# A third depth for bursts of value products in a planned two-layer attention kernel

## The chip, the cores and the metric

The kernel runs on one core of a Trainium2 chip. The metric is the device time in microseconds of one execution; the kernel before takes 1564.23 us in the median of 3 runs (1563.62 to 1565.77).

## What is computed

Two rounds of attention and MLP over 2048 tokens of width 512, with the same weights in both rounds. Attention has 32 heads of width 16, so the score matrix is large for the little that each head computes: 32 x 2048 x 2048 exponentials in each round.

```python
def _A_ref(x, wqkv, wo):               # S = 2048, D = 512, H = 32, Dh = 16
    qkv = (x @ wqkv).reshape(B, S, 3, H, Dh).transpose(2, 0, 3, 1, 4)
    q, k, v = qkv[0], qkv[1], qkv[2]
    scores = einsum("bhqd,bhkd->bhqk", q, k) * Dh ** -0.5
    o = einsum("bhqk,bhkd->bhqd", softmax(scores), v)
    return o.transpose(0, 2, 1, 3).reshape(B, S, D) @ wo

def _B_ref(x, w1, b1, w2, b2):         # F = 1376
    return gelu(layernorm(x) @ w1 + b1) @ w2 + b2

x = x + _A_ref(layernorm(x), wqkv, wo)
x = x + _B_ref(layernorm(x), w1, b1, w2, b2)
# and both once more; inputs and weights are bf16
```

## The kernel before

**The work.** Each round's attention is cut into segments: a block of up to 512 queries times a group of four heads. A segment's scores are made in tiles of 128 keys x 512 queries for one head (`score`, L1466 to L1471): K is the stationary operand, and as a head fills only 32 rows of the array, four heads sit side by side in four row tiles. There are 4,096 such tiles in the program. A tile becomes probabilities in one of two ways:

- ScalarE (ACT) takes a group of three or two tiles and writes `exp` into the buffers `PT` (L1455). Groups alternate between PSUM banks 0 to 2 and 3 to 4, so that one group is computed while the other is read.
- VectorE (DVE) turns a tile into the bits of an exponential by adding a constant and converting to a 16-bit integer, into `dp` (L1555). It adds three shifted copies, two tiles at a time (L1588), and the four are averaged by multiplying with V scaled to match. Such a tile makes four value products instead of one. Only key blocks 3, 6, 9, 12 and 15 may go this way.

The value products (`try_pv`, L1605 to L1664) multiply probabilities with V (17 columns: 16 of the head and one of ones for the denominator). Four heads sit in four column tiles of the array, all adding into PSUM bank 6 (`ACCB`). Scores need the array in row tiles, value products in column tiles, projections and MLP the whole array; PE goes from one to the other in turns. When a segment's products are all in, DVE transposes the bank (L1688), and the next segment may start to add.

**Who sets the order.** The program is made by a planner, in Python, before anything runs: `Sched` keeps pending tasks for each engine, estimates when each could start, and emits them one by one with priorities. Scores have priority 0.0, value bursts 1.0. `best` and `scores_due` hold back a task of lower priority on PE when it would end later than scores that ACT will soon need, by `HOLD_LATE`. After the planning, `refill` puts matmuls on zeros (L1359, L1361, L1363) into PE's gaps to keep its clock up.

**A value burst.** `try_pv` looks at the products that are ready or will be within `PV_NEAR`, sorts them by column tile, and picks a depth r, the number of products per column tile in this burst, by the largest value. The burst goes out if the value reaches `PV_LEAST`, if score groups lack a `PT` buffer (`starved`), if the segment's last products are there, or if PE will have stood idle for half a microsecond. At most two bursts wait on PE at a time.

```python
value = lambda r: sum(min(r, len(v)) for v in by.values()) / (4.0 * (r + PV_COST))
r = max(range(1, PV_DEEP + 1), key=value)
if value(r) < HINT.PV_LEAST and not self.starved and len(near) < sg["n"] - sg["sub"]:
```

**The settings.** Class `Hint` (L506 to L519) holds a base setting and variations of it, one field or so in each. `ORDER` is a string of digits, one for every eight score groups: `flow_scores` (L1387) counts groups in `gi` and calls `HINT.at(gi // 8)`, which resets the base and applies the variation of that digit. So the string steers, stretch by stretch, when tiles go to DVE (`D_IDLE`, `D_STEAL`), how full a value burst must be (`PV_LEAST`), how early products count as ready (`PV_NEAR`), how far scores may be delayed (`HOLD_LATE`), and the priority of the second half of projections (`LIN2`). The depth limit `PV_DEEP` is a constant, 2.

Of the kernel before, what the change touches and what calls it, by code (L numbers as in the profile page):

```python
# [267 lines left out]
def I(fn, reads=(), writes=(), dur=0.3, same_ok=(), lat=None):  # L268
    return (fn, tuple(reads), tuple(writes), tuple(same_ok), dur, lat)
# [230 lines left out]
MISCB = 7  # L500
DTAIL = 8
DURGE = 8
PV_DEEP = 2
PV_COST = 0.5
PV_IDLE = 0.5


class Hint:
    BASE = dict(D_IDLE=1.2, PV_LEAST=0.75, HOLD_LATE=0.4, PV_NEAR=0.7, LIN2=9, D_STEAL=0)
    MODES = (dict(), dict(D_IDLE=0.8), dict(D_IDLE=1.7), dict(PV_LEAST=0.6), dict(PV_LEAST=0.9), dict(HOLD_LATE=0.2), dict(HOLD_LATE=0.6), dict(PV_NEAR=0.4), dict(LIN2=0.9), dict(D_STEAL=1.0))  # L510
    STEP = 8
    ORDER = '0355550015621021500127723542380000551183094330404202738042440023535555121020004212005090903453421320027044075009578104471100282939255971103200420580357499912000'

    def mode(self, k):
        self.__dict__.update(self.BASE)
        self.__dict__.update(self.MODES[k])

    def at(self, step):
        self.mode(int(self.ORDER[step], 36) if step < len(self.ORDER) else 0)  # L519


HINT = Hint()
# [3 lines left out]
class Builder:  # L526
# [1078 lines left out]
    def try_pv(self):  # L1605
        S_ = self.S_
        while True:
            if self.acc_seg >= len(self.segs) or not self.acc_free:
                return
            sg = self.segs[self.acc_seg]  # L1610
            if self.pv_out >= (1 if self.pv_first else 2) or not sg["rdy"]:
                return
            near = [it for it in sg["rdy"] if self.P.last_writer[it[2]].t1 <= S_.now + HINT.PV_NEAR]
            if len(near) < len(sg["rdy"]):
                S_.seq += 1
                heapq.heappush(S_.timers, (min(self.P.last_writer[it[2]].t1 for it in sg["rdy"] if it not in near) - HINT.PV_NEAR + 0.01, S_.seq, self.try_pv))
            if not near:
                return
            by = defaultdict(list)
            for it in near:  # L1620
                by[sg["tiles"][it[1]][1]].append(it)
            value = lambda r: sum(min(r, len(v)) for v in by.values()) / (4.0 * (r + PV_COST))
            r = max(range(1, PV_DEEP + 1), key=value)
            if value(r) < HINT.PV_LEAST and not self.starved and len(near) < sg["n"] - sg["sub"]:
                t = self.P.drain + PV_IDLE
                if S_.now < t or self.pv_out:
                    if not self.pv_timer:
                        self.pv_timer = True
                        S_.seq += 1
                        heapq.heappush(S_.timers, (max(t, S_.now) + 0.01, S_.seq, self.pv_again))  # L1630
                    return
            turns = [[v[k] for v in by.values() if len(v) > k] for k in range(r)]
            pick = [it for turn in turns for it in turn]
            for it in pick:
                sg["rdy"].remove(it)
            sg["sub"] += len(pick)
            nfirst = len(sg["first"])
            ops = []
            nth = {}
            for k, turn in enumerate(turns):  # L1640
                for it in turn:
                    nth[it[1], it[5]] = k
            for (s_, j, res, ap, use, sh) in pick:
                kbs, hp = sg["tiles"][j]
                hg, W, q = sg["hg"], sg["W"], sg["qslot"]
                first = hp not in sg["first"]
                sg["first"].add(hp)
                if first and sg["nparts"] == 2:
                    first = False
                    ops.append((nth[j, sh] - 0.1, I(lambda e, hp=hp, q=q: e.matmul(self.ps[32 * hp:32 * hp + 18, ACCB, :], lhsT=self.rsel[:, hp, :], rhs=self.QT[:, q, :], start=True, stop=False, skip_group_check=True, tile_position=(0, 32 * hp)),  # L1650
                                                     [("rsel",), ("qt", q)], [("ps", ACCB)], W / 2400.0, [("ps", ACCB)], ("col", hp))))
                for i, kb in enumerate(kbs):
                    if sh:
                        d = sg["dks"].index(kb) + sg["doff"]
                        v, RV = self.vs[:, q, sh - 1, d, 17 * hp:17 * hp + 17], ("vs", q, d)
                    else:
                        v, RV = self.V[:, hg, kb, hp, :], ("V", hg, kb)
                    ops.append((nth[j, sh] + 0.1 * i, I(lambda e, hp=hp, v=v, ap=ap[:, i * W:(i + 1) * W], first=first and i == 0, W=W: e.matmul(  # L1658
                        self.ps[32 * hp:32 * hp + 17, ACCB, 0:W], lhsT=v, rhs=ap, start=first, stop=False, skip_group_check=True, tile_position=(0, 32 * hp)),
                                     [res, RV], [("ps", ACCB)], W / 2400.0, [("ps", ACCB)], ("col", hp))))  # L1660
            ops = [o for i, o in sorted(ops, key=lambda x: x[0])]
            self.pv_first = nfirst < 4
            self.pv_out += 1
            S_.submit(Task("pe", 1.0, ops), cb=lambda sg=sg, pick=pick: self.pv_done(sg, pick))  # L1664
# [354 lines left out]
```

## Time and profile before

| what | from the profile of the kernel before |
|---|---|
| span of the profiled run | 1564.7 us, 39,699 instructions |
| exp groups on ACT (L1455) | 1,273, 1433.7 us: 590 of three tiles (1515 ns) and 683 of two (1086 ns, some overlap) |
| tiles on DVE (L1555) | 960, mean 679 ns |
| shifted copies on DVE (L1588) | 1,428 of 1,024 columns, mean 430 ns, and 24 of 512 |
| score matmuls (L1470) | 4,608 |
| value products (L1658) | 7,857 |
| zero matmuls (L1359, L1361, L1363) | 487, 465 and 1,808 |
| DMA | 24.9% of 16 engines' time on the main queue |

The page gives the busy time of each engine: PE for matmuls and PEld for their weight loads, DVE, ACT, POOL. "L1455 ACT ... idle before <-PE ps L1470" reads: the instructions of line 1455 found ACT idle before them, and what they waited for in the end was a matmul of line 1470. The chain that ended last is followed back from the last instruction, each step to what released it. A turn is here a run of matmuls in one tiling of the array, row tiles, column tiles or the whole, until the next turn's first matmul.

### The profile page before, as it was taken

To read this page: it belongs to the slowest core of one execution; us is meant where nothing else is said; L and a number is where in the kernel's file an instruction comes from. 1 tells how busy PE (TensorE), PEld (TensorE's weight loads), DVE (VectorE), ACT (ScalarE), POOL (GpSimd) and SP (SyncE) were. 2 spreads that over 40 slices of the span, in tenths; PEclk is the share of its full clock that TensorE was granted. 3 is DMA by queue.
4 is the path that set the end of the run, shared out by engine and by line. 5 is a ranking of instruction groups with operands and counts; after the bars stand their busy time and mean duration, and the time that the engine had idled before them with its cause. 6 is when DMAs were issued, how large, how long until landed. Compare 5 with 4: busy or idle time off the path is not lost.

```text
span 1564.7 us, 39699 instructions
## 1 busy us (share of the span) xinstructions
PE 1517.7 (97%) x16674; PEld 483.1 (31%) x16674; DVE 1459.9 (93%) x3256; ACT 1517.1 (97%) x1361; POOL 321.2 (21%) x558
## 2 busy tenths in 40 slices
PE   9999999999999999999999999999999999999998
PEld 3222222232223222222222322222232232344444
DVE  7699999999999899989999799999899999999894
ACT  8979999999999999999999999999999999999996
POOL 3575312001210021203222227410001000020100
PEclk9999999999999999999999999999999999999999
DMA  7663111203311232223832232310102000211110
GB/s 162 116 143 97 35 31 32 61 17 85 85 40 46 47 76 59 61 48 92 145 45 66 56 82 63 62 25 22 35 16 44 22 17 25 41 45 32 43 30 19
DMA packets 212451, 88.69 MB, mean 57 GB/s; under 512 B 183307, under 2 KB 207152, under 8 KB 212272
## 3 DMA queue, kind: packets, MB, share of 16 engines
q1 hardware_dynamic: 212272, 86.16, 24.9%
q8 instruction: 130, 2.13, 0.6%
q14 instruction: 49, 0.40, 0.1%
HBM read 34.65 MB, written 19.48 MB: 35 GB/s over the span
## 4 chain that ended last, share of the span: by engine, by line
ACT 34%; DVE 33%; PE 29%; issue 2%; POOL 1%; SPq 1%; DMA 1%; POOLq 0%; DVEq 0%
ACT PT L1455 33%; DVE dp L1555 13%; DVE dp L1588 10%; PE ps L1470 9%; PE ps L1658 8%; PE ps L1835 3%; PE ps L1792 2%; PE ps L950 2%; DVE accT L1688 2%; DVE n L1015 1%; ACT h L1827 1%; PE ps L1359 1%; DVE sq L991 1%; DVE h L1816 1%; PE ps L1068 1%
## 5 line engine op out<-in xcount | busy, mean ns | idle before, releaser
L1455 ACT ACTIVATE PT<-ps 128x1536 bf16<-128x1536 f32 (+1 forms) x1273 | 1433.7, 1285 | 28.5 <-PE ps L1470 25.1
L1555 DVE TENSOR_SCALAR dp<-ps 128x512 uint16<-128x512 f32 x960 | 638.1, 679 | 36.7 <-PE ps L1470 34.2
L1470 PE MATMUL ps<-QT,KT 32*128 32x512 bf16 (+1 forms) x4608 | 599.1, 359 | 19.6 <-ACT PT L1455 6.8
L1588 DVE TENSOR_SCALAR dp<-dp 128x1024 uint16<-128x1024 uint16 (+1 forms) x1452 | 559.9, 427 | 4.6 <-PE ps L1658 1.6
L1658 PE MATMUL ps<-PT,V 128*17 128x512 bf16 (+1 forms) x3525 | 483.8, 358 | 0.2 <-ACT PT L1455 0.2
L1658 PE MATMUL ps<-dp,vs 128*17 128x512 bf16 (+1 forms) x3249 | 467.6, 357 | 0.9 <-DVE dp L1588 0.4
L1470 PEld LDWEIGHTS ps<-QT,KT 32*128 32x128 bf16 x4608 | 161.1, 91 | 545.9 <-ACT PT L1455 286.3
L1196 POOL TENSOR_SCALAR QT<-qraw,scl,qbias 128x512 bf16<-128x512 bf16 (+1 forms) x83 | 72.3, 872 | 764.6 <-PE ps L1470 758.1
L1658 PE MATMUL ps<-dp,V 128*17 128x512 bf16 (+1 forms) x1083 | 227.1, 358 | 1.6 <-DVE accT L1688 0.6
L1363 PE MATMUL ps<-zw 128*32 128x448 bf16 (+23 forms) x1808 | 172.2, 321 | 0.8 <-DVE dp L1555 0.7
L1658 PEld LDWEIGHTS ps<-dp,vs 128*17 128x17 bf16 x3249 | 119.1, 88 | 115.4 <-issue 87.2
L1658 PEld LDWEIGHTS ps<-PT,V 128*17 128x17 bf16 x3525 | 116.9, 88 | 92.8 <-issue 78.5
L1361 PE MATMUL ps<-zw 32*128 32x444 bf16 (+5 forms) x465 | 132.8, 317 | 0.0
L1359 PE MATMUL ps<-zw 128*128 128x448 bf16 (+17 forms) x487 | 114.7, 334 | 3.2 <-DVE onec L754 2.1
L1792 PE MATMUL ps<-yT,wf 128*128 128x512 bf16 (+3 forms) x396 | 101.7, 361 | 3.1 <-DVE dp L1588 1.3
L950 PE MATMUL ps<-wqkv,xnT 128*128 128x512 bf16 x336 | 93.4, 382 | 5.8 <-DVE dp L963 2.2
L1363 PEld LDWEIGHTS ps<-zw 128*32 128x32 bf16 x1808 | 62.5, 95 | 27.8 <-DVE dp L1555 4.6
L1658 PEld LDWEIGHTS ps<-dp,V 128*17 128x17 bf16 x1083 | 55.5, 88 | 41.4 <-issue 24.1
L1221 POOL TENSOR_SCALAR vs<-V 128x340 bf16<-128x340 bf16 (+2 forms) x72 | 61.8, 859 | 26.1 <-PE ps L1658 15.1
L1688 DVE STREAM_TRANSPOSE accT<-ps 128x512 f32<-128x512 f32 (+1 forms) x88 | 57.8, 657 | 7.1 <-PE ps L1658 7.0
L1816 DVE TENSOR_SCALAR h<-ps,b1c 128x512 bf16<-128x512 f32 (+2 forms) x88 | 61.9, 703 | 1.9 <-PE ps L1792 1.5
L1359 PEld LDWEIGHTS ps<-zw 128*128 128x128 bf16 x487 | 37.6, 98 | 64.7 <-issue 40.0
(182 smaller groups left out, 885.5 us busy)
## 6 DMA issues: line engine op xcount, KB each, us to landing
vs<-vs_scr SPq DMA_DIRECT2D x56, 255.0 KB, 2.7
wf<-in_B_w_dram SPq DMA_DIRECT2D x90, 128.0 KB, 2.9
q_scr<-qk SPq DMA_DIRECT2D x20, 256.0 KB, 2.1
k_scr<-qk SPq DMA_DIRECT2D x12, 256.0 KB, 2.0
out_dram<-xres SPq DMA_DIRECT2D x16, 128.0 KB, 1.8
vs_scr<-vs SPq DMA_DIRECT2D x8, 255.0 KB, 2.9
xres<-in_A_x_dram SPq DMA_DIRECT2D x7, 256.0 KB, 3.2
v_scr<-vst SPq DMA_DIRECT2D x12, 136.0 KB, 1.7
```

Of the source, the lines that this page charges most:

```text
L950: yield Task("pe", prio if c0 == 0 else min(prio, HINT.LIN2), [I(lambda e, c=c: e.matmul(self.ps[:, b, :], lhsT=xnT[:, c, :], rhs=self.wqk ...
L1359: fn = lambda e: e.matmul(self.ps[:, b, 0:w], lhsT=self.zw[:, 0:128], rhs=self.zw[:, 0:w], start=st, stop=st, skip_group_check=True)
L1361: fn = lambda e: e.matmul(self.ps[:, b, 0:w], lhsT=self.zw[32 * p:32 * p + 32, 0:128], rhs=self.zw[32 * p:32 * p + 32, 0:w], start=st, sto ...
L1363: fn = lambda e: e.matmul(self.ps[32 * p:32 * p + 32, b, 0:w], lhsT=self.zw[:, 0:32], rhs=self.zw[:, 0:w], start=st, stop=st, skip_group_c ...
L1455: S_.submit(Task("act", 1e-5 * gi, [I(lambda e, pt=pt, n=n, b0=b0: e.activation(out=self.PT[:, pt:pt + n, :], in_=self.ps[:, b0:b0 + n, :] ...
L1470: return [I(lambda e, kb=kb, i=i: e.matmul(self.ps[:, b, i * W:(i + 1) * W], lhsT=self.KT[32 * hp:32 * hp + 32, hg, kb * 128:(kb + 1) * 12 ...
L1555: self.S_.submit(Task("dve", 0.0, [I(lambda e: e.tensor_scalar(out=self.dp[:, u, w * 512:(w + 1) * 512], in0=self.ps[:, b, :], scalar1=BIT ...
L1588: yield Task("dve", pr, [I(lambda e, k=k, v=v: e.tensor_scalar(out=self.dp[:, v, 0:N], in0=self.dp[:, u, 0:N], scalar1=float(SHIFT[k]), sc ...
L1658: ops.append((nth[j, sh] + 0.1 * i, I(lambda e, hp=hp, v=v, ap=ap[:, i * W:(i + 1) * W], first=first and i == 0, W=W: e.matmul(self.ps[32 ...
L1688: yield Task("dve", 0.3, [I(lambda e: e.transpose(self.accT[:, a, 0:W], self.ps[:, ACCB, 0:W]), [("ps", ACCB)], [RA], 0.17 + 0.535 * W / 5 ...
L1792: yield Task("pe", pr if c0 == 0 else min(pr, HINT.LIN2), [I(lambda e, c=c: e.matmul(self.ps[0:M, b, off:off + W], lhsT=self.w1(fc, c), rh ...
L1816: S_.submit(Task("dve", pr - 0.7, [I(lambda e, fc=fc, M=M, b=b: e.tensor_scalar(out=hv[0:M, fc * W:(fc + 1) * W], in0=self.ps[0:M, b, 0:W] ...
```

## The change

The depth limit becomes one of the fields that a setting may change. The base keeps 2. Two settings are added: a (a depth of 3), and b (a depth of 3, and a burst must reach a value of 0.84). The digits are read in base 36, so a and b need no new reading. The string of settings is a new one; its first 15 characters are as before, and from there on 127 of 145 differ. Twelve are a and fifteen are b. A burst of three per column tile lets PE change between row and column tiles less often.

```diff
-PV_DEEP = 2
 PV_COST = 0.5
 PV_IDLE = 0.5
 
 class Hint:
-    BASE = dict(D_IDLE=1.2, PV_LEAST=0.75, HOLD_LATE=0.4, PV_NEAR=0.7, LIN2=9, D_STEAL=0)
-    MODES = (dict(), dict(D_IDLE=0.8), dict(D_IDLE=1.7), dict(PV_LEAST=0.6), dict(PV_LEAST=0.9), dict(HOLD_LATE=0.2), dict(HOLD_LATE=0.6), dict(PV_NEAR=0.4), dict(LIN2=0.9), dict(D_STEAL=1.0))
+    BASE = dict(D_IDLE=1.2, PV_LEAST=0.75, HOLD_LATE=0.4, PV_NEAR=0.7, LIN2=9, D_STEAL=0, PV_DEEP=2)
+    MODES = (dict(), dict(D_IDLE=0.8), dict(D_IDLE=1.7), dict(PV_LEAST=0.6), dict(PV_LEAST=0.9), dict(HOLD_LATE=0.2), dict(HOLD_LATE=0.6), dict(PV_NEAR=0.4), dict(LIN2=0.9), dict(D_STEAL=1.0), dict(PV_DEEP=3), dict(PV_DEEP=3, PV_LEAST=0.84))
     STEP = 8
-    ORDER = '0355550015621021500127723542380000551183094330404202738042440023535555121020004212005090903453421320027044075009578104471100282939255971103200420580357499912000'
+    ORDER = '035555001562102a7b002a10378140b0a9b4400b2720a3048043b939400a433b43a0040b145523b7a110030b029922bb701ab0305733aa8531874000a09424434b380315000205ba188933009b003120'
...
-            r = max(range(1, PV_DEEP + 1), key=value)
+            r = max(range(1, HINT.PV_DEEP + 1), key=value)
```

## The prediction

> **What bounds the kernel now.** I read the profile from the outside in: the busy shares, then the span cut in three, then who waits for whom in the middle piece, then the chain of waits there.
>
> The first part of the page and the two lines of its chain:
>
> ```profile
> PE 1517.7 (97%) x16674; PEld 483.1 (31%) x16674; DVE 1459.9 (93%) x3256; ACT 1517.1 (97%) x1361; POOL 321.2 (21%) x558
> ...
> ACT 34%; DVE 33%; PE 29%; issue 2%; POOL 1%; SPq 1%; DMA 1%; POOLq 0%; DVEq 0%
> ACT PT L1455 33%; DVE dp L1555 13%; DVE dp L1588 10%; PE ps L1470 9%; PE ps L1658 8%; PE ps L1835 3%; PE ps L1792 2%; PE ps L950 2%; DVE accT L1688 2%; DVE n L1015 1%; ACT h L1827 1%; PE ps L1359 1%; DVE sq L991 1%; DVE h L1816 1%; PE ps L1068 1%
> ```
>
> Three engines are nearly full and the chain hops between them in equal parts, so no single one "is" the bound. PE's 97% contains zero matmuls that keep it warm (L1359, L1361, L1363: 115, 133 and 172 us, partly beside real work), so PE has slack in the sum, though not at every moment. ACT has none to speak of: it idles 47 us in all.
>
> Where? The setting of the burst depth is read anew every eight score groups from a string of 160 characters, and the new string first differs at character 15, so at group 120. In the trace the 120th exp (counted from 0) starts at 158.2 us. The last exp ends at 1543.6 us. So I cut there (columns: stage, length, then busy time of PE, weight loads, DVE, ACT, POOL, the clock, the DMA share, GB/s):
>
> ```profile
> 0.00:158.00 158.00, 148.47 (x1210) 46.29 (x1214) 133.27 (x310) 142.23 (x149) 85.54 (x179) 1.00 0.60 128
> 158.00:1543.60 1385.60, 1352.83 (x15364) 427.49 (x15360) 1320.71 (x2934) 1367.91 (x1200) 234.18 (x375) 1.00 0.22 49
> 1543.60:1564.70 21.10, 16.42 (x108) 9.30 (x108) 5.88 (x13) 7.01 (x14) 1.48 (x4) 1.00 0.04 13
> ```
>
> The head of 158 us can't change, and the tail of 21.1 us is a fixed string of projection, norm and MLP after the last segment. In the middle ACT idles 1385.6 - 1367.9 = 17.7 us and DVE 64.9 us. That is all there is to be won without cutting work. Who ends these waits, in the middle piece (us in total, times, longest):
>
> ```profile
> PEld ps L1470 <- ACT PT L1455: 260.1, 671, 0.9
> ...
> DVE dp L1555 <- PE ps L1470: 33.3, 50, 2.8
> ...
> ACT PT L1455 <- PE ps L1470: 14.1, 33, 2.4
> ...
> DVE dp L1588 <- PE ps L1658: 1.6, 7, 0.3
> ```
>
> The scores' weight load mostly waits for an exp to free its banks: ACT sets the pace. ACT itself waits for scores only 33 times, DVE 50 times. The last line is important for the buffers: DVE almost never waits for value products to free a `dp` buffer, and no line has ACT waiting for a value product at all.
>
> One gap is of another kind. Between 1213.0 and 1217.5 us the granted clock is 0.62 and ACT is busy 2.37 of 4.5 us:
>
> ```profile
> 1213.00:1217.50 4.50, 4.06 (x27) 1.00 (x27) 2.12 (x5) 2.37 (x3) 0.77 (x1) 0.62 0.00 0
> ```
>
> **What a burst costs.** Where PE is on the chain, the turns can be read off it (start, us, what):
>
> ```profile
> 1098.24 0.32 PE ps L1470 x3
> 1098.56 0.54 PE ps L1658 x8
> 1099.10 0.32 PE ps L1470 x3
> 1099.43 0.54 PE ps L1658 x8
> 1099.97 0.54 PE ps L1835 x2
> ```
>
> and elsewhere on it
>
> ```profile
> 337.38 0.97 PE ps L1658 x16
> ```
>
> Eight products (two per column tile) take 0.54 us from start to the next turn, sixteen take 0.97 us, so a level of four costs 0.215 us and a change of turn 0.11 us. The trace also has 14 unmixed turns of twelve, median 0.76 us, just on that line. Three per tile therefore occupies PE for 0.76 us instead of 0.54.
>
> **What the Trainium skill says.** "TensorEngine Tiling (Array Packing)", section Key Properties: a change of tiling mode, not of tile alone, drains the engine. The trace agrees, 0.11 us a change, which is the whole mechanical ground of the edit. "TensorE: Matmul & The Clock Gate", section Back-to-back issue gap, gives 512/2.4 + 2.5 ns = 216 ns a matmul; the level here is 0.215 us. The same page, Part 1, says that after about 3.4 us with too little activity the array clock halves; the dip at 1213 us is the only one of the middle piece, so it bears on the chances, not on the sum. "Perfetto Trace Analysis", section Identifying the Most-Contended Engine, says that matmul busy time isn't a measure of PE; here too, with zero matmuls in it.
>
> **The change, part by part.**
>
> 1. `PV_DEEP` becomes a field of the settings, 2 by default: no instruction changes, nothing to price.
>
> 2. Settings a and b (depth 3; b also asks a value of at least 0.84). The burst's value is (products)/(4(r+0.5)): 8 of 8 at depth 2 give 0.80, 12 of 12 at depth 3 give 0.857, 11 give 0.786. Under a, depth 3 wins with twelve ready, and eight ready still go. Under b only a full twelve goes, unless PE has stood for 0.5 us or a buffer is missing. They stand at 27 of the 145 characters from 15 on, 19% of the middle. The middle has 7,548 value products in 803 column turns, counted in the trace: 1,887 levels, 2.35 per turn (487 turns of two, 147 of four, that is two bursts in a row, 60 of three). In 19%: 351 levels, now in 149 turns. With bursts of three, some still doubled or cut short, I take 3.2 levels a turn: 110 turns, 39 fewer. Each saves 0.11 us, and at most another 0.11 if the score turn between falls away too: 4.3 to 8.6 us of PE. What lies on the path? The page has PE on 29% of the chain: 1.2 to 2.5 us. I take 2.
>
> 3. What the deeper burst makes wait. Behind a value burst on PE stand the next scores, and behind those ACT. ACT frees its banks at the end of an exp and then works on the other group: a pair of groups takes 2.27 us (19 exps in 21.55 us from 699 us on), about 1.02 us for the short group and 1.25 to 1.45 for the long one. A turn of 0.54 and a score turn of 0.33 make 0.87, below 1.02: hidden. 0.76 + 0.33 = 1.09 is 0.07 above the short one and hidden by the long one. Two bursts of three in a row, 1.41 + 0.33 = 1.74, show in either case, by 0.3 to 0.7 us. The planner's rule that holds back what would end after the scores are due guards against that; that four-level turns (0.97 + 0.33 = 1.30) occur 147 times and ACT waits only 33 times shows that the rule works. I put this at +0.5 us in the forecast case.
>
> 4. Buffers. Waiting for twelve rather than eight: products come at 7,548/1385.6 = 5.4 per us, so 0.7 us longer. `PT` has 22 usable slots against 2.2 tiles per us, ten microseconds' worth, and the lines above show no engine waiting for value products beyond 1.6 us. Hidden; 0.
>
> 5. The rest of the string. From character 15 on 127 of 145 characters differ, 100 of them with none of the new settings. They remove and add no instruction as such; they shift when score tiles go to DVE instead of ACT and when products are put off. Price: a tile moved from ACT to DVE saves ACT 1433.7/3136 = 0.457 us (3,136 = 590 x 3 + 683 x 2 tiles) and costs DVE 0.679 + 1.5 x 0.430 = 1.32 us. If a share f of both idle times is filled, DVE: 64.9 f = d + 1.32 m; ACT: 17.7 f = d - 0.457 m. This gives m = 26.5 f tiles and d = 29.8 f us. The ceiling is 30 us. Nothing in the profile fixes f; 147 turns of four show that bursts already run together, so much of the new freedom is there already. I choose f = 0.09, about 2.7 us, from bounds of -0.2 and +0.4.
>
> Sum: 2 - 0.5 + 2.7 = 4.2 us. 1564.2 - 4.2 = 1560.0 us.
>
> **The rivals.** *Off the path*: PE's slack swallows parts 2 and 5. For it: 260 us of score loads waiting for ACT against 14 us of ACT waiting for scores. Against it: 33% of the chain is DVE, which waits 33 us for score tiles. Time 1564. *Longer bursts hurt*: the 110 deep turns come in pairs as often as bursts do now ((147 + 20)/803, a fifth): 22 pairs at 0.3 to 0.7 us, 7 to 15 us, half held off by the rule, and another 2 us because DVE's tiles queue behind the same burst. About +6 us, 1570. For it: most of the larger ACT gaps in the trace follow a turn of sixteen or full-array matmuls of the MLP. Against it: the same trace has few of them. *More is filled*: the clock dip, whose gaps cost ACT 1.78 + 0.56 + 0.39 = 2.7 us, goes away, and f reaches 0.2 (6 us), with part 2 on top: about 11 us, 1553.5.
>
> **How the numbers follow.** Forecast case 0.48, more filled 0.14, off the path 0.18, hurt 0.20. The forecast case spreads over 1557 to 1563; 0.2% is 3.1 us, so four fifths of it count as faster: 0.39 + 0.14, and a little of the off-path case, 0.55. Same: the rest of these, 0.24. Slower: 0.21. The range from 1551 to 1571 takes in the centre of each rival and leaves out one in ten on either side.
>
> **What would show it.** The first 120 exps as before, the 121st still at 158.2 us. Column turns after it down from 803 to about 760, turns of three up from 60 to about 120. ACT's idle time in the middle a little below 17.7 us, DVE tiles (L1555) at 960 to 966. Wrong, if the turns fall and the time doesn't (off the path), if ACT's wait for L1470 grows well over 14 us (bursts in the way), or if the L1555 count moves by ten or more, for then the balance, not the depth, set the time.

## The result

The changed kernel takes 1573.09 us (median of 4 executions, 1569.41 to 1577.09), the kernel before 1563.92 us beside it. The ratio is 1.0057, with a 95% interval from 1.0031 to 1.0083: slower by 9 us, where 4 us less was forecast, and above the range given. The times of the changed kernel also lie 8 us apart, those of before 2 us. Below, the clock of an execution is the mean TensorE clock granted to it, as a share of the full one.

### The profile page after: what moved, and what is told of

Read it like the earlier page. It is cut to its first block, busy times and chain, and to the rows that moved or that the text cites. A ratio compares the mean times of both kernels' runs of the same rounds, so it can differ in the third digit from the quotient of the medians.

```text
span 1567.6 us, 39691 instructions
## 1 busy us (share of the span) xinstructions
PE 1506.6 (96%) x16585; PEld 485.9 (31%) x16717; DVE 1463.4 (93%) x3257; ACT 1517.7 (97%) x1361; POOL 312.0 (20%) x558
## 4 chain that ended last, share of the span: by engine, by line
PE 35%; ACT 30%; DVE 30%; issue 2%; DMA 1%; POOL 1%; SPq 0%; POOLq 0%; DVEq 0%
ACT PT L1454 29%; DVE dp L1554 12%; PE ps L1469 11%; PE ps L1657 10%; DVE dp L1587 9%; PE ps L1834 4%; PE ps L1791 3%; PE ps L1358 2%; PE ps L949 2%; DVE accT L1687 1%; PE ps L1362 1%; DVE h L1815 1%; DVE n L1014 1%; ACT h L1826 1%; PE ps L1736 1%
## 5 line engine op out<-in xcount | busy, mean ns | idle before, releaser
L1469 PE MATMUL ps<-QT,KT 32*128 32x512 bf16 (+1 forms) x4608 | 606.7, 360 | 16.8 <-DVE dp L1554 3.5
L1657 PE MATMUL ps<-PT,V 128*17 128x512 bf16 (+1 forms) x3523 | 493.9, 358 | 0.0
L1195 POOL TENSOR_SCALAR QT<-qraw,scl,qbias 128x512 bf16<-128x512 bf16 (+1 forms) x83 | 68.8, 829 | 793.1 <-PE ps L1469 787.5
L1362 PE MATMUL ps<-zw 128*32 128x448 bf16 (+20 forms) x1838 | 180.8, 321 | 0.2 <-DVE dp L1554 0.2
L1360 PE MATMUL ps<-zw 32*128 32x444 bf16 (+7 forms) x483 | 140.1, 317 | 0.0
L1358 PE MATMUL ps<-zw 128*128 128x448 bf16 (+22 forms) x476 | 111.9, 337 | 2.9 <-DVE onec L753 2.1
L1791 PE MATMUL ps<-yT,wf 128*128 128x512 bf16 (+3 forms) x358 | 93.8, 359 | 9.6 <-issue 4.6
L949 PE MATMUL ps<-wqkv,xnT 128*128 128x512 bf16 x299 | 86.1, 382 | 11.0 <-issue 4.2
L1362 PEld LDWEIGHTS ps<-zw 128*32 128x32 bf16 x1838 | 66.3, 95 | 25.3 <-DVE dp L1554 5.1
```

The lines of the kernel that those rows point to most:

```text
L949: yield Task("pe", prio if c0 == 0 else min(prio, HINT.LIN2), [I(lambda e, c=c: e.matmul(self.ps[:, b, :], lhsT=xnT[:, c, :], rhs=self.wqk ...
L1358: fn = lambda e: e.matmul(self.ps[:, b, 0:w], lhsT=self.zw[:, 0:128], rhs=self.zw[:, 0:w], start=st, stop=st, skip_group_check=True)
L1360: fn = lambda e: e.matmul(self.ps[:, b, 0:w], lhsT=self.zw[32 * p:32 * p + 32, 0:128], rhs=self.zw[32 * p:32 * p + 32, 0:w], start=st, sto ...
L1362: fn = lambda e: e.matmul(self.ps[32 * p:32 * p + 32, b, 0:w], lhsT=self.zw[:, 0:32], rhs=self.zw[:, 0:w], start=st, stop=st, skip_group_c ...
L1469: return [I(lambda e, kb=kb, i=i: e.matmul(self.ps[:, b, i * W:(i + 1) * W], lhsT=self.KT[32 * hp:32 * hp + 32, hg, kb * 128:(kb + 1) * 12 ...
L1791: yield Task("pe", pr if c0 == 0 else min(pr, HINT.LIN2), [I(lambda e, c=c: e.matmul(self.ps[0:M, b, off:off + W], lhsT=self.w1(fc, c), rh ...
```

## The profile after

The profiled execution is the shortest of the four, a span of 1567.6 us, 2.9 us over the span of before. The profile of before is the other way round: it is of an execution of 1566.5 us, 2.6 us above the median of 1563.92, and has a halving of the clock in it, while 56 of the 63 executions of that kernel in the experiments below have a clock of 1.000. So the two profiles lie closer together than the two medians. The busy times and the chain, from the page of the changed kernel (its lines stand one higher than before, 1454 for 1455 and so on):

```profile
PE 1506.6 (96%) x16585; PEld 485.9 (31%) x16717; DVE 1463.4 (93%) x3257; ACT 1517.7 (97%) x1361; POOL 312.0 (20%) x558
...
PE 35%; ACT 30%; DVE 30%; issue 2%; DMA 1%; POOL 1%; SPq 0%; POOLq 0%; DVEq 0%
ACT PT L1454 29%; DVE dp L1554 12%; PE ps L1469 11%; PE ps L1657 10%; DVE dp L1587 9%; PE ps L1834 4%; PE ps L1791 3%; PE ps L1358 2%; PE ps L949 2%; DVE accT L1687 1%; PE ps L1362 1%; DVE h L1815 1%; DVE n L1014 1%; ACT h L1826 1%; PE ps L1736 1%
...
L1454 ACT ACTIVATE PT<-ps 128x1536 bf16<-128x1536 f32 (+1 forms) x1273 | 1434.3, 1275 | 30.0 <-PE ps L1469 26.4
L1554 DVE TENSOR_SCALAR dp<-ps 128x512 uint16<-128x512 f32 x961 | 638.6, 679 | 36.3 <-PE ps L1469 33.2
```

ACT works about as long as before (1517.7 against 1517.1 us) and idles 2.3 us longer. DVE takes 961 score tiles, one more; it is busy 3.5 us longer, and its idle time is as before (104.2 and 104.8 us). The stages cut as before (the third to the span's end):

```profile
0.00:158.00 158.00, 147.55 (x1206) 46.77 (x1221) 135.38 (x312) 143.10 (x150) 85.19 (x179) 1.00 0.58 128
158.00:1543.60 1385.60, 1340.14 (x15244) 428.70 (x15356) 1322.08 (x2933) 1365.01 (x1196) 225.30 (x375) 1.00 0.22 49
1543.60:1568.00 24.40, 18.88 (x146) 10.41 (x141) 5.95 (x14) 9.60 (x17) 1.47 (x4) 0.97 0.07 21
```

ACT's idle time in the middle is 20.6 us where it was 17.7. Two waits stand out. The first lies in the second attention layer, where its first block of queries goes from the first twelve key blocks to the last four. The scores from there on need a bound worked out from all sixteen key blocks (`scl`). In ACT's order of time (start, length, what, idle before), first the changed kernel, then the one before:

```profile
929.05 9.50 ACT L1454 ACTIVATE PT<-ps 128x1536 bf16<-128x1536 f32 x8 [0.23 <-PE ps L1469]
942.53 8.23 ACT L1454 ACTIVATE PT<-ps 128x1536 bf16<-128x1536 f32 x7 [3.98 <-PE ps L1469]
```

```profile
928.84 11.62 ACT L1455 ACTIVATE PT<-ps 128x1536 bf16<-128x1536 f32 x10 [0.16 <-PE ps L1470]
941.22 9.31 ACT L1455 ACTIVATE PT<-ps 128x1536 bf16<-128x1536 f32 x8 [0.76 <-PE ps L1470]
```

The bound itself, first in the changed kernel, then in the one before:

```profile
940.88 0.23 DVE L1165 TENSOR_SCALAR scl<-ps,onesm 128x8 f32<-128x8 f32 x1 [0.27 <-PE ps L1164]
```

```profile
940.99 0.23 DVE L1166 TENSOR_SCALAR scl<-ps,onesm 128x8 f32<-128x8 f32 x1 [0.27 <-PE ps L1165]
```

It comes at the same time in both. In both the chain ahead of it is mostly DVE, with tiles and copies among the key norms, and then POOL. ACT of the changed kernel had got ahead: its last exp of the old kind ends at 938.55 us, and the one at 942.53 is the first with new scores. In the kernel before, the exp at 941.22 still takes the last three score tiles of the old kind (2,430 to 2,432 of the 4,096, counted in the trace), and the first with new scores follows at 942.66 without a wait. So the wait of 3.98 us gives up a lead, but doesn't put the changed kernel behind. What does comes after it: from the first new exp to the last of all the changed kernel needs 603.6 us (942.53 to 1546.17), the one before 600.9 (942.66 to 1543.56). With 0.3 us in the tail, less the 0.1 us of lead, that is the 2.9 us.

The second wait is on PE. In the order of time of the changed kernel:

```profile
1403.05 1.49 PE L1791 MATMUL ps<-yT,wf 128*128 128x512 bf16 x3 [1.99 <-DMA yT<-xn]
1404.58 0.75 DVE L1815 TENSOR_SCALAR h<-ps,b1c 128x512 bf16<-128x512 f32 x1 [2.45 <-PE ps L1791]
1405.13 1.45 ACT L1454 ACTIVATE PT<-ps 128x1536 bf16<-128x1536 f32 x1 [2.79 <-PE ps L1469]
```

The first MLP matmul of a token block stands in PE's queue ahead of scores and value products, and waits 1.99 us for the DMA that transposes its input. Everything behind it waits too, and at 1402.9 us the granted clock falls to half for 3.4 us, so that even the following matmuls are slow. In the stretch around it the mean clock is 0.62 and ACT busy less than half:

```profile
1402.50:1407.00 4.50, 3.95 (x37) 1.26 (x42) 2.35 (x5) 1.87 (x2) 0.00 (x0) 0.62 0.07 15
```

The kernel before has a like event at 1213.7 us, shown in the prediction, after a stand of PE of 1.34 us.

As for the bursts: counted in the trace from 158 us to 1543.6 us, turns of three levels rose from 60 to 89, turns of four fell from 147 to 123, turns of one rose from 89 to 125, and all column turns from 803 to 827. Some bursts became longer, others were broken up; the pairs of strings further below, which differ in depth alone, have fewer turns with the greater depth, so the rise is put down to the rest of the plan.

## The experiments

Three theories. **Bursts**: deeper bursts put off scores and DVE tiles, and so cost the time. **Clock**: single stands of PE trip the clock, and how many do differs from one execution to the next. **Order**: neither; the string of settings is fitted, character by character, to one plan. Each character changes the plan behind it, and the new string is simply fitted less well.

### The clock

The changed kernel once more, unedited.

> The changed kernel once more, unedited, for its spread and for a second trace. Clock theory (PE stands still at single places, the array clock halves for 3.4 us there, and how often differs from execution to execution): times spread over 6 us or more, from about 1567 to 1577, and the longer an execution the lower its mean clock, some 2 to 3 us for each 0.001. Burst theory (deeper bursts put scores and DVE tiles off): the delay is in every execution alike, spread under 3 us, a median near 1573, no relation to the clock.

Measured: 1570.76 us (1568.78 to 1574.99), ratio 1.0049 (1.0036 to 1.0061). The five executions and their mean clocks: 1568.78 at 1.000, 1570.57 and 1570.76 at 0.999, 1573.09 at 0.998, 1574.99 at 0.997. So 2.1 us for each 0.001, as the clock theory says. The profiled one has a second halving at 281.2 us that the earlier trace lacks, after a stand of PE of 2.12 us. Its first exp with new scores starts at 945.83 us where the earlier trace has 942.53, 3.3 us later; 0.3 us of these were there at the 120th exp, and 2.9 us come in by the 240th (from 295.1 to 298.3 us), which is the price of the stand and the halving together. But the execution at clock 1.000 still takes 1568.8 us, 5 us over the median of before. So time and clock go together in these five, and the base of the loss is not the clock.

Both kernels with more zero matmuls; every other instruction keeps its place on its engine:

```diff
-FILL_U = 0.55
+FILL_U = 0.70
```

> The changed kernel with the target of zero matmuls raised from 0.55 to 0.70 (3,409 of them planned where there were 2,797; the order of all other instructions is the same on every engine). Clock theory: fewer halvings, median 1564 to 1567, spread under 4 us. Burst theory: 1571 to 1575 as before or a little more, since zero matmuls move no score. Order theory (the new string simply gives a worse plan): unchanged too.

> The kernel before with the same raised target (3,382 zero matmuls, 2,760 before; all else in the same order). It has one halving of the clock in its trace, at 1214 us. Clock theory: that one goes or stays, so 1561 to 1564. Burst and order theories: 1564, no change. If the added zero matmuls themselves cost time, it is seen here: over 1566.

Measured: the changed kernel 1571.9 us (1568.42 to 1573.31), ratio 1.0047 (1.0034 to 1.0061); the kernel before 1562.96 us (1562.38 to 1564.01), ratio 0.9992 (0.9984 to 1.0). In neither trace is there a halving within the span. The same 4.5 us that cost the kernel before so much are whole with the added zero matmuls:

```profile
1213.00:1217.50 4.50, 4.50 (x49) 1.30 (x51) 4.50 (x12) 4.41 (x5) 0.80 (x1) 1.00 0.15 33
```

From its exp at 941.32 us (941.22 before) to the last one it takes 599.8 us in place of 602.3, so this event cost 2.5 us. That the zero matmuls removed it isn't shown, for PE's stand ahead of it is gone too, first before, then with more zero matmuls:

```profile
1213.44 1.61 PE L1792 MATMUL ps<-yT,wf 128*128 128x512 bf16 x4 [1.34 <-DVE dp L1588]
```

```profile
1212.54 0.81 PE L1792 MATMUL ps<-yT,wf 128*128 128x512 bf16 x3 [0.16 <-DVE dp L1555]
```

The changed kernel, however, was expected at 1564 to 1567 by the clock theory and stays near 1572, although four of its five executions have a clock of 1.000; these four alone spread from 1568.4 to 1572.1. So the clock isn't the whole of the spread either, and the four give no sign that the median falls with the halvings gone.

Between the two traces without a halving, the changed kernel is 5.7 us longer (1567.7 and 1562.0). The exps at the bound, changed kernel first:

```profile
943.98 11.41 ACT L1454 ACTIVATE PT<-ps 128x1536 bf16<-128x1536 f32 x10 [3.98 <-PE ps L1469]
```

```profile
941.32 12.91 ACT L1455 ACTIVATE PT<-ps 128x1536 bf16<-128x1536 f32 x11 [0.76 <-PE ps L1470]
```

The first with new scores starts 1.2 us later (943.98 and 942.75; the one at 941.32 again takes the last old tiles), from there to the last exp it takes 602.3 against 598.4 us, and the tail is 0.5 us longer. ACT idles 4.4 us more in all (49.3 and 44.9), DVE 2.8 us more (104.9 and 102.1). So the larger part of the loss is not the clock. Why the filled kernel still spreads by 4 us at a clock of 1.000, only one of its traces being at hand, stays open.

### The depth

The two new settings with a depth of 2, the string as it is:

```diff
-... dict(PV_DEEP=3), dict(PV_DEEP=3, PV_LEAST=0.84))
+... dict(PV_DEEP=2), dict(PV_DEEP=2, PV_LEAST=0.84))
```

> The changed kernel with a depth of 2 in the settings a and b, and nothing else edited; b then asks 0.84, which a burst of two per tile never reaches, so under it bursts go only when PE idles or a buffer is missing. Burst theory: back at 1562 to 1566. Order theory: stays at 1569 to 1576, as the string is still the new one. Clock theory: any value between 1562 and 1576, following the mean clock.

Measured: 1602.48 us, ratio 1.0249 (1.0235 to 1.0263). All three theories missed it. Taking the deep bursts out of 27 of 160 characters made the kernel 30 us slower, not faster. That speaks against the burst theory, but says nothing for the depth: b at depth 2 is a different and harsh setting, and the plan behind the first a is another one. The order theory had foreseen too little: it took the string for 10 us better or worse, not 30. So I tried strings that were fitted to nothing, in pairs that differ in depth alone.

```diff
+    ORDER = '0' * 160                          # e5_all_base
+    ORDER = 'a' * 160                          # e6_all_deep
+    ORDER = '035555001562102' + '0' * 145      # e7_head_base
+    ORDER = '035555001562102' + 'a' * 145      # e8_head_deep
```

> The changed kernel with a string of 160 zeros: the base setting, a depth of 2, throughout. Order theory (a string is good only for the one plan in which each of its characters was chosen, and either string is worth tens of microseconds): far above both kernels, 1590 to 1615. Burst theory (what made the change slow is the deeper burst): 1564 to 1572, as there is no deep burst in it and one setting in a hundred can't be worth much.

> A string of 160 times the setting a: base with a depth of 3 throughout. Burst theory: slower than the string of zeros by far more than the 9 us of the change, which has the depth in 17% of its characters only, so by 20 to 50 us. Order theory: anywhere within 15 us of the string of zeros, above or below.

> The 15 characters that both strings share, then zeros. Order theory: within 15 us of the string of zeros. Burst theory: 1564 to 1572.

> The same 15 characters, then the setting a. Burst theory: slower than the same head with zeros by 20 to 50 us, as in the other pair. Order theory: the difference of this pair has no fixed sign; a depth of 3 may be faster in one pair and slower in the other, by some 5 to 10 us.

Measured, with the ratio to the kernel before, and counts from the traces (turns between 158 and 1543.6 us):

| string | us | ratio and interval | column turns | of three levels | tiles on DVE |
|---|---|---|---|---|---|
| all base | 1607.15 | 1.0282 (1.0262 to 1.0302) | 808 | 45 | 938 |
| all a | 1596.87 | 1.0205 (1.0185 to 1.0225) | 759 | 113 | 951 |
| head, base | 1600.69 | 1.0235 (1.0215 to 1.0255) | 798 | 50 | 942 |
| head, a | 1608.29 | 1.0277 (1.0257 to 1.0297) | 752 | 132 | 942 |

Here the depth does what it was meant to: 6% fewer column turns in both pairs, and more than twice as many of three. The time goes down by 10.3 us in one pair and up by 7.6 in the other. Two pairs don't give a mean, but they show, on strings that were fitted to nothing, that a depth of 3 has no fixed sign, and that the burst theory's 20 to 50 us are not there. They also show what a string is worth: the base setting throughout costs 43 us against the kernel before. The page of the string of zeros tells where these lie:

```profile
PE 1538.8 (96%) x16672; PEld 490.1 (31%) x16799; DVE 1450.9 (90%) x3207; ACT 1535.3 (96%) x1367; POOL 317.1 (20%) x558
...
L1454 ACT ACTIVATE PT<-ps 128x1536 bf16<-128x1536 f32 (+1 forms) x1279 | 1452.0, 1267 | 45.9 <-PE ps L1469 40.1
L1554 DVE TENSOR_SCALAR dp<-ps 128x512 uint16<-128x512 f32 x938 | 625.8, 680 | 55.0 <-PE ps L1469 51.7
L1587 DVE TENSOR_SCALAR dp<-dp 128x1024 uint16<-128x1024 uint16 (+1 forms) x1425 | 555.9, 428 | 21.4 <-PE ps L1657 16.6
```

ACT waits 17.4 us longer ahead of its exps than in the kernel before (45.9 and 28.5), DVE 18.3 us longer ahead of its tiles (55.0 and 36.7). DVE takes 22 tiles fewer, which ACT has to do (22 x 0.457 = 10 us of the 18.2 us that it is longer busy). The last line is a wait that the kernel before hardly has (1.6 us): DVE's copies wait 16.6 us for value products, which free a `dp` buffer. With all a it is 10.7 us, in the other pair 15.1 and 16.0, so it goes with the badly fitted string and not with the depth. In these traces, then, a string's tens of microseconds are waits of two engines, and tiles that ACT has to take over.

### One character

The string of the kernel before with its 24th character (counted from 0), 3, replaced: once by the old setting 0, once by the new a.

```diff
-'035555001562102150012772 3 54238...'
+'035555001562102150012772 0 54238...'     # e11_one_char_old
+'035555001562102150012772 a 54238...'     # e12_one_char_deep
```

(The blanks only set the character off.)

> The kernel before with one character of its string changed, the 24th (counted from 0) from 3 to 0: one old setting for another, for eight score groups, no deep burst anywhere. Order theory: the plan from there on is another one and the remaining 135 characters no longer fit it, so 15 to 45 us slower than before. Burst theory: within 3 us of before.

> The same character from 3 to a, so a depth of 3 for eight groups and nowhere else. Order theory: as slow as the other one-character edit, within 10 us of it. Burst theory: the deep setting costs a few microseconds at most in so short a stretch, the other edit nothing.

Measured: 1590.61 us, ratio 1.0169 (1.0153 to 1.0184), and 1598.13 us, 1.0222 (1.0206 to 1.0237). One old setting in place of another, for eight of 1,273 groups and with no deep burst anywhere, costs 26 us, and the deep one 34. The page of the first:

```profile
L1454 ACT ACTIVATE PT<-ps 128x1536 bf16<-128x1536 f32 (+1 forms) x1275 | 1442.8, 1253 | 41.8 <-PE ps L1469 36.0
L1554 DVE TENSOR_SCALAR dp<-ps 128x512 uint16<-128x512 f32 x957 | 637.2, 679 | 42.8 <-PE ps L1469 39.9
```

The same picture as with the string of zeros: more waits of both engines. Eight groups are only 9 us of ACT's work in all (8 x 1.13), and the trace shows that the loss isn't in them. Counted in score tiles done by ACT and DVE, against the kernel before with more zero matmuls, this run is 0.2 us behind at tile 768 (319 us), past the eight groups, 11 us at tile 2,048 and 25 us at the last. So the time is lost little by little in the plan behind the edited character, as it would be if the 135 characters there no longer fit. It is one place in the string, edited twice; other places were not tried.

### Strings fitted afresh

Two strings, both chosen in one way, over all twelve settings and over the ten old ones: character by character, keeping at each step the sixteen beginnings that leave the least work for ACT and DVE by the planner's own account. How the strings of the two kernels were chosen is not on record.

```diff
+ORDER = '0055555b125aab3bb332734b44b414a4ab9b410455239b4ab943a54b734055452355ba552235423aaa733bb015542a5b373331b75353954a5550b122b05473449535550333ba49522599843585b98353'   # e9_search12
+ORDER = '0055855553027533210373335520055855393005050040365412505400514430930351557550552732327559539230714304103312144548595402123124322948205594310715031599922595089352'   # e10_search10
```

> A third string, chosen character by character over all twelve settings: at each step the sixteen best beginnings are kept, by what the planner estimates of the work then left on ACT and DVE. 33 of its 160 characters are a or b, more than the 27 of the changed kernel. Order theory: a string chosen for its own plan is good whatever depth it uses, so 1555 to 1566. Burst theory: as many deep bursts as in the changed kernel, so 1569 or more.

> The same choice over the ten old settings alone, so no burst of a depth of 3. Order theory: within 5 us of the string chosen over twelve, on either side. If a depth of 3 is worth something to a string that is fitted to it, the string over twelve is the faster by more than 3 us; if it costs, by the burst theory, the slower by 5 or more.

Measured, 21 executions each: 1562.1 us with deep bursts, ratio 0.9984 (0.9978 to 0.9991); 1561.7 us without, ratio 0.9982 (0.9976 to 0.9989). Both are faster than both kernels, and 0.4 us from each other, which one string of each kind can't tell from nothing. The first has 797 column turns, 116 of three levels, more than the 89 of the changed kernel; the second has 820 and 62. The burst theory wanted 1569 or more for the first. The page of the second:

```profile
PE 1515.9 (97%) x16609; PEld 482.8 (31%) x16609; DVE 1465.5 (94%) x3275; ACT 1513.5 (97%) x1361; POOL 319.8 (21%) x558
...
L1454 ACT ACTIVATE PT<-ps 128x1536 bf16<-128x1536 f32 (+1 forms) x1273 | 1429.4, 1289 | 25.3 <-PE ps L1469 22.6
L1554 DVE TENSOR_SCALAR dp<-ps 128x512 uint16<-128x512 f32 x964 | 640.8, 679 | 30.7 <-PE ps L1469 28.3
```

The fair trace to put beside it is that of the kernel before with more zero matmuls, which has no halving either in its middle (1562.0 us, and this one 1559.4). ACT waits as long ahead of its exps in both (25.3 and 25.6 us), and is busy 3.6 us less here (1513.5 and 1517.1); four tiles more on DVE account for 1.8 us of that (4 x 0.457). The gap at the bound is there too:

```profile
939.73 10.06 ACT L1454 ACTIVATE PT<-ps 128x1024 bf16<-128x1024 f32 x9 [3.31 <-PE ps L1469]
```

but this first exp with new scores comes at 939.7 us, 2.8 us ahead of the changed kernel, as the bound is ready at 938.1 us (940.9 there). So a wait of ACT at this place isn't a loss by itself; what counts is when the bound is ready.

The planner has an account of its own. It is Python in the kernel and keeps a start and an end for each instruction that it places, and in every trace the exps and the DVE tiles come in the order that it planned. The ends are estimates, worked out from the kernels' code after the runs, and not measurements. The last one comes at 1549.5 us for the kernel before and at 1555.3 us for the changed kernel: 5.8 us more, where the two traces without a halving differ by 5.7. For the string of zeros it comes 44.2 us later than before (43.0 measured), for the one old character 30.3 us (26.1 measured), for the two strings fitted afresh 4.0 and 5.7 us earlier (2.4 and 2.8 measured). So the loss of the changed kernel, but for what the clock and the waits for DMA may add, is in its plan already. "Fitted less well" says no more than that: the plan is the longer one.

## Why the prediction was wrong

**The step that failed is the fifth of the change**, "the rest of the string". It priced 127 changed characters as a small push on the idle times, a share f of 0.09, 2.7 us, with bounds of -0.2 and +0.4. It let the characters shift when tiles go to DVE and when products are put off, and had no price for what an edit does to the plan behind it. The runs showed something else: the one character that was tried is worth 26 us in the kernel before, and all of them together are worth 43 us against the base setting, because each edit changes the plan behind it. So the right question was whether the new string gives as good a plan as the old one. Nothing in the diff or in the profile of before answers that, but the planner does, by 5.8 us the wrong way. In the terms of the sum, the 4.2 us to be won in all turned into about 5.7 us lost between the two traces without a halving of the clock. With the other steps as forecast that is -7.2 us for this one, a share f of -0.24, outside its own bounds.

**The second step, the value of fewer turns**, was put at 2 us with 39 turns fewer. It failed too, but is the smaller term. The level of 0.215 us and the change of turn of 0.11 us were right (unmixed turns of twelve are 0.76 us in the changed kernel too, 32 of them). But the number of turns went up by 24, since the rest of the plan moves it more than the depth does. Where the depth alone was changed, turns did fall by 46 to 49, and the time went either way by 8 to 10 us.

**The third and fourth steps**, what stands behind a deeper burst and what it holds in buffers, at +0.5 and 0 us: no run shows a cost of depth. Between the traces without a halving, ACT's wait for scores in the middle rose from 10.7 to 14.6 us, and 3.2 us of that is the one wait at the bound (0.76 and 3.98). In the freshly fitted string with the most deep settings it is 12.8 us. DVE's copies wait 0.6 us for value products in the changed kernel, 1.6 before. One reading under the third step was wrong: turns of four aren't always two bursts in a row. Of the 105 unmixed turns of sixteen matmuls in the middle of before, 60 hold matmuls of 256 columns, two to a product, and are one burst; the median of all is 0.55 us, that of the other 45 is 0.975. That the rival "longer bursts hurt" had 1570 us, close to the measured time, is chance. Its cause isn't what happened.

**The clock** was named only among the rivals, as a gain of 2.7 us if the one halving went. The price of such an event was about right (2.5 us in one place, 2.9 in another, the stand of PE included). But the gain wasn't there to be had: the halving was in the profiled execution, and most executions of that kernel have none, by their clock of 1.000. What was missed is that a plan may have several places on the brink. Only one of nine executions of the changed kernel has a clock of 1.000, and the lowest, 0.996, stands for about four halvings (an estimate: 3.4 us at half clock are 0.0011 of this span). That goes with the spread; how much of the median it makes isn't shown, since the run with more zero matmuls, four of five at 1.000, has a median of 1571.9 us. The Trainium skill, "TensorE: Matmul & The Clock Gate", section "HAM oscillation — how this bites in real kernels", describes PE going cold in a wait for a DMA, and asks for no idle gap over some 3.4 us. The trace agrees that a wait for a DMA stands ahead of the halving, but differs on the length: the clock fell at 1402.9 us, 1.8 us into a stand of 1.99 us, with PE busy 1.59 of the 3.41 us before.

**The forecasts of what would show it**: the first 120 exps are as before, and the 121st starts at 157.2 us (158.2 before). Turns about 760: 827. Turns of three about 120: 89. ACT's idle time below 17.7 us: 20.6. DVE tiles 960 to 966: 961. The sign that was named for "the balance set the time", a count of DVE tiles off by ten, fails to show in the changed kernel: its loss is not in the share of the tiles.

What stays open: which of the 127 characters are the weak ones, which decisions of the plan cost the 3.9 us after the bound, and how much of the 9 us in the median, past the 5.7 us in the two traces, is the clock and how much the waits for DMA that come ahead of it.

## What to carry to other kernels

When a change replaces a fitted table of settings, don't price it by what its entries do; edit one entry of the old table first, and see how far the time moves. If it moves by more than the effect that you are after, the new feature can only be judged with the table fitted anew with and without it, as here, where strings fitted afresh gained 2.4 and 2.8 us and the depth nothing that could be seen. Where a planner keeps times of its own, compare its two plans before anything else. See also whether the profile that a forecast starts from is of a typical execution; here it held a halving that most executions lack. And where a queue is filled ahead of time, look for the instruction that waits for a DMA in front of work that the bounding engine needs.

## What the runs showed of the hardware

After 1.8 us of a stand of PE of 1.99 us, in a wait for a DMA, the granted clock fell to half for 3.4 us. The length of a stand alone doesn't tell: past the first 20 us the traces of all runs hold four stands of 1.77 us or more, each followed by a halving, and twelve of 1.21 to 1.65 us, of which four were and eight weren't; two halvings (at 190.1 us with the head and all a, at 1580.8 us with all a) have no stand over 1.2 us near them. With more zero matmuls four of five executions of the changed kernel had a clock of 1.000, without them one of nine. One halving with the stand ahead of it cost 2.5 us in one place and 2.9 in another. In five executions of one kernel the time followed the mean clock at 2.1 us for each 0.001, while with more zero matmuls it spread over 3.7 us at one and the same clock.
